# One fixed TensorE order in an attention stage: parts of one tile mode next to each other, zero-padded last rows, operations over two heads

## Chip, cores and metric

The program runs on one core of one Trainium2 chip. The metric is the device time of one execution in microseconds (us). Before the change it is 1012.68 us, the median of 3 runs (1012.34 to 1013.3).

## What is computed

Attention by feature maps, and behind it two feed-forward layers. The change lies in the attention alone; its shapes are 4 batches, 8 heads, 576 positions and a head size of 64, with 128 features.

```python
def phi(x):
    proj = np.einsum('bhsd,df->bhsf', x, w_phi)
    proj = proj - np.max(np.abs(proj), axis=-1, keepdims=True)
    return np.concatenate([np.exp(proj), np.exp(-proj)], axis=-1)
q_p, k_p = (phi(q), phi(k))
kv = np.einsum('bhsf,bhsd->bhfd', k_p, v)
z = np.sum(k_p, axis=2)
num = np.einsum('bhsf,bhfd->bhsd', q_p, kv)
den = np.einsum('bhsf,bhf->bhs', q_p, z)[..., None] + 1e-06
x = num / den            # then tokens x 512
x = relu(x @ w_in)**2 @ w_out
x = (sigmoid(x @ w_gate) * (x @ w_val)) @ w_out2
```

## The kernel before

The attention is a loop of 16 iterations, n = 0 to 15, one for each pair of heads (4 batches, NJ = 4 pairs each). An iteration touches three pairs at once, as a software pipeline: it transposes q and k of pair n+2 (`trans`, lines 298, 305 and 313), projects pair n+1 (`proj_k` line 347, `proj_q` line 326), forms the key sums of pair n (`kv`: line 373 for k_p times v, line 380 for the sums z by a column of ones) and transposes them (`kv_tr`, line 390), and forms denominators (line 403) and numerators (line 410) of pair n-1 (`num`). Of the 576 keys of a head, 512 are four chunks of 128 rows; the other 64 (the "last rows") of eight heads are packed two by two into the 128 partitions of `vr` and of the tile `phr`, and each pair of heads uses one half of these partitions.

The operands do not fill the TensorE array, so its instructions work on parts of it. The profile writes the part of an instruction as rows*columns: `128*64` means that two independent column halves exist, `128*32` four column quarters, `64*128` two row halves. Below this is called the tile mode. Each plain fp32 matmul of the program is two MATMUL instructions in the trace; an fp32r matmul and a transpose are one.

The other engines serve these matmuls. ScalarE (ACT) copies results out of PSUM (lines 289, 329, 382, 383, 392) and takes the exponentials (lines 338, 339 for q, 354, 355 for k). VectorE (DVE) subtracts the high part of a transposed tile (line 290), finds and subtracts maxima (lines 352, 353, and line 337 for q), transposes the denominators (line 414), inverts them (416, 417), spreads them (427) and multiplies (430). GpSimd (POOL) finds the maxima for q over partitions (line 331) and moves the inverted denominators (line 424). For q these operations act on half a head (288 columns), for k on one head (512 columns). In ten of the iterations (`CONVERTING`) DVE also runs one weight conversion of four operations of 512 columns (lines 111 to 116) for the feed-forward part; in four others it splits a part of the attention's result into high and low (`xsplit`, lines 95 and 96).

PSUM has eight one-bank tiles of 512 columns in this stage (`bank`). The order of instructions on each engine is set while the program is built, by a scheduler that follows the order of the code as far as data and buffers allow in its own model; at run time each engine takes its instructions strictly in that order. `tc.issue_after` puts an instruction behind another one of the same engine. Behind the loop the attention's PSUM tiles are given back and the feed-forward part begins at line 530.

Of the kernel before, what the change touches and what calls it, by code (L numbers as in the profile page):

```python
# [19 lines left out]
def attention_moe_moe2(ctx, tc, q, k, v, w_phi, w_in, w_out, w_gate, w_val, w_out2, out):  # L20
# [196 lines left out]
    with ExitStack() as actx:  # L217
# [25 lines left out]
        ones = cst.tile([P, 32], F32, name="ones")  # L243
        nc.vector.memset(ones, 1.0)
# [14 lines left out]

        nat = {}  # L260

        def load_rem(b):
# [3 lines left out]
            vr = lv.tile([P, 2, 2, D], F32, tag="vr", name="vr", bufs=2)  # L266
            for a in range(2):
                nc.sync.dma_start(out=vr[a * SR:(a + 1) * SR].rearrange("p g e d -> p (g e) d"),
                                  in_=v[b, 4 * a:4 * a + 4, SM:S, :].rearrange("h p d -> p h d"))
# [17 lines left out]
        def split_evac(pst, nm, key, bufs):  # L287
            t = tp.tile([P, 2, pst.shape[1]], F32R, tag=nm, name=nm, bufs=bufs)
# [4 lines left out]
        def trans_k(b, j):  # L293
            pt = bank(512)
            a = nat["k", b, j]
            for c in range(4):
                e, r = divmod(c, 2)
                nc.tensor.transpose(pt[:, c * P:(c + 1) * P], a[:, e, 2 * r:2 * r + 2, :], ident)  # L298
            split_evac(pt, "kT", ("k", b, j), 2)

        def trans_q(b, h):
            pt = bank(SH)
            a = nat["q", b, h // 2]
            for r in range(3):
                nc.tensor.transpose(pt[:, r * P96:(r + 1) * P96], a[:, h % 2, 2 * r:2 * r + 2, :], ident[:P96, :P96])  # L305
            split_evac(pt, "qT", ("q", b, h), 4)

        def trans_rem(b):
            a = nat["kr", b]
            pt = bank(NJ * SR)  # L310
            for j in range(NJ):
                o = (j % 2 * 2 + j // 2) * SR
                nc.tensor.transpose(pt[:, o:o + SR], a[:, 2 * j:2 * j + 2, :], ident[:SR, :SR])
# [4 lines left out]


        def proj_q(b, h):  # L320
            t = tT["q", b, h]
            pps = [bank(SH) for e in range(2)]
            for n, (x, y) in enumerate(passes):
                for e in range(2):
                    sl = slice(e * D, (e + 1) * D)
                    nc.tensor.matmul(pps[e], lhsT=wq[sl, x, :], rhs=t[sl, y, :], start=n == 0, stop=n == 2)  # L326
            for e in range(2):
# [4 lines left out]
                qx[b, h, e] = a  # L332
                mx[b, h, e] = m

        def q_exp(b, h, e):
            a = qx[b, h, e]
            nc.vector.tensor_tensor(a[:, 1, :], a[:, 1, :], mx[b, h, e], ALU.subtract)
# [5 lines left out]
        def proj_k(t, o, key, tag, bufs):  # L343
            pp = bank(512)
            for r in range(2):
                for n, (x, y) in enumerate(passes):
                    nc.tensor.matmul(pp[:, r * 256:(r + 1) * 256], lhsT=t[:, x, o + r * P:o + (r + 1) * P],  # L347
                                     rhs=wk[:, y].rearrange("p a f -> p (a f)"), start=n == 0, stop=n == 2)
            a = pp.rearrange("p (c f) -> p c f", c=4)
            t = php.tile([P, 4, 2, F], F32, tag=tag, name=tag, bufs=bufs)  # L350
# [503 lines left out]
```

## Time and profile before

| | us |
|---|---|
| median of 3 runs | 1012.68 |
| the profiled execution | 1013.1 |
| its span in the profile | 1011.3 |
| attention stage, up to the first matmul of line 530 | 198.4 |
| the rest | 812.9 |
| TensorE busy in the span | 991.6 (98%) |
| VectorE busy in the span | 747.3 (74%) |
| ScalarE busy in the span | 601.7 (59%) |

The profile shows one execution. A line of a timeline gives the start, the duration from the first start to the last end, the engine (PE is TensorE's matmuls, PEld its weight loads), the line of the kernel, the operation and its operands, and in brackets the idle time before it and what ended that. Instructions of one engine overlap a little at their ends, so the price of a group on a busy engine is the distance from its start to the start of the next. A line of the windows gives the window, its length, the busy time and, in brackets, the instructions of PE, PEld, DVE, ACT and POOL in this order, the granted TensorE clock (1.00 is 2.4 GHz, and the lower level, 1.2 GHz, is 0.50), the share of the DMA engines and GB/s.

### The profile page before, as it was taken

How to read it: one execution, taken by the hardware profiler on the slowest of the kernel's cores; microseconds unless marked ns; L12 is line 12 of the kernel's file. 1: busy time of each engine (PE TensorE's matmuls, PEld its weight loads, DVE VectorE, ACT ScalarE, POOL GpSimd, SP SyncE). 2: the span in 40 equal slices, each digit the busy share in tenths (PEclk: the TensorE clock that was granted, in tenths of full speed). 3: DMA queues.
4: the chain of work that ended last, by engine and by line, in shares of the span. 5: the costliest groups of instructions: out<-in, count | busy, mean ns of one | idle time of the engine just before them, and what ended most of it. 6: DMA issues, size and time to landing. Idle time of an engine off the chain costs nothing.

```text
span 1011.3 us, 17524 instructions
## 1 busy us (share of the span) xinstructions
PE 991.6 (98%) x6488; PEld 870.3 (86%) x6488; DVE 747.3 (74%) x1296; ACT 601.7 (59%) x1081; POOL 109.7 (11%) x196
## 2 busy tenths in 40 slices
PE   7999999999999999999999999999999999999996
PEld 6666666599999999889998899998899988999985
DVE  6799998869885987986969769856565656566532
ACT  6888878556555786446864466654465644555431
POOL 4556655400000000000000000000000000000000
PEclk9999999999999999999999999999999999999999
DMA  9444521349984576565775556632444422544302
GB/s 236 127 134 141 160 76 57 113 156 351 304 293 141 183 254 191 167 200 186 260 226 171 177 167 205 189 118 74 118 142 133 124 77 64 166 125 135 96 11 62
DMA packets 116406, 159.56 MB, mean 158 GB/s; under 512 B 12768, under 2 KB 74848, under 8 KB 116320
## 3 DMA queue, kind: packets, MB, share of 16 engines
q1 hardware_dynamic: 115680, 157.58, 49.8%
q8 instruction: 51, 0.84, 0.3%
q10 hardware_dynamic: 640, 0.85, 0.2%
q14 instruction: 35, 0.29, 0.1%
HBM read 125.37 MB, written 33.03 MB: 157 GB/s over the span
## 4 chain that ended last, share of the span: by engine, by line
PE 94%; DVE 3%; ACT 2%; POOL 0%; issue 0%; ACTq 0%
PE d L603 38%; PE d L551 20%; PE d L707 15%; PE d L530 7%; PE a L373 3%; PE a L410 3%; PE a L347 2%; PE a L380 2%; PE a L403 2%; PE a L326 1%; PE a L305 1%; PE a L390 1%; PE a L298 1%; ACT qe L329 0%; PE a L258 0%; ACT c L609 0%
## 5 line engine op out<-in xcount | busy, mean ns | idle before, releaser
L603 PE MATMUL d<-xs,hl 128*128 128x384 f32 x2184 | 385.4, 337 | 3.6 <-ACT c L609 3.6
L603 PEld LDWEIGHTS d<-xs,hl 128*128 128x128 f32 x2184 | 379.4, 188 | 6.6 <-ACT c L609 4.9
L138 DVE TENSOR_TENSOR hl<-wf,hl 128x512 fp32r<-128x512 f32 x282 | 192.4, 687 | 75.5 <-ACT hl L137 74.5
L137 ACT ACTIVATE hl<-wf 128x512 fp32r<-128x512 f32 x282 | 175.0, 626 | 88.5 <-PE d L603 48.3
L551 PE MATMUL d<-ghi,hl 128*128 128x256 f32 (+1 forms) x768 | 190.7, 338 | 0.0
L551 PEld LDWEIGHTS d<-ghi,hl 128*128 128x128 f32 x768 | 131.8, 188 | 16.3
L551 PE MATMUL d<-glo,hl 128*128 128x512 f32 (+1 forms) x384 | 128.5, 338 | 0.0
L707 PE MATMUL d<-hl,ghi 128*128 128x512 f32 x432 | 126.7, 395 | 0.0
L93 ACT ACTIVATE ghi<-G 128x768 fp32r<-128x768 f32 x48 | 40.7, 847 | 99.3 <-PE d L707 56.0
L707 PEld LDWEIGHTS d<-hl,ghi 128*128 128x128 f32 x432 | 80.9, 188 | 18.2
L96 DVE TENSOR_TENSOR glo<-G,ghi 128x768 fp32r<-128x768 f32 x48 | 46.0, 958 | 57.4 <-ACT ghi L93 56.9
L609 ACT ACTIVATE c<-d 128x768 f32<-128x768 f32 x78 | 61.3, 809 | 44.8 <-PE d L603 44.6
L331 POOL PARTITION_ALL_REDUCE m<-qe x64 | 83.5, 1375 | 35.5 <-ACT qe L329 33.3
L632 DVE TENSOR_TENSOR c<-c,d 128x768 f32<-128x768 f32 x54 | 51.2, 953 | 41.1 <-ACT c L609 26.8
L551 PEld LDWEIGHTS d<-glo,hl 128*128 128x128 f32 x384 | 72.3, 188 | 8.6
L707 PE MATMUL d<-hl,glo 128*128 128x512 f32 x216 | 76.3, 395 | 0.0
L530 PE MATMUL d<-xs,hl 128*128 128x384 f32 x384 | 69.1, 337 | 0.0
L530 PEld LDWEIGHTS d<-xs,hl 128*128 128x128 f32 x384 | 66.7, 188 | 1.1 <-issue 0.4
L115 ACT ACTIVATE st<-st 128x512 f32<-128x512 f32 x68 | 45.5, 678 | 32.4 <-DVE w L112 29.8
L707 PEld LDWEIGHTS d<-hl,glo 128*128 128x128 f32 x216 | 40.6, 188 | 9.8
L112 DVE SCALAR_TENSOR_TENSOR w<-st,w 128x512 uint32<-128x512 uint32 x68 | 46.6, 698 | 0.2
L113 DVE SCALAR_TENSOR_TENSOR w<-st,w 128x512 uint32<-128x512 uint32 x68 | 46.4, 693 | 0.5
(109 smaller groups left out, 1134.4 us busy)
## 6 DMA issues: line engine op xcount, KB each, us to landing
wf<-wd SPq DMA_DIRECT2D x84, 256.0 KB, 3.0
wf<-smd SPq DMA_DIRECT2D x72, 256.0 KB, 3.1
st<-in_moe_w_out_dram SPq DMA_DIRECT2D x28, 512.0 KB, 5.2
wf<-gvd SPq DMA_DIRECT2D x54, 256.0 KB, 3.2
wf<-wid SPq DMA_DIRECT2D x46, 256.0 KB, 4.3
st<-in_moe_w_in_dram SPq DMA_DIRECT2D x16, 512.0 KB, 5.9
wf<-ismd SPq DMA_DIRECT2D x32, 256.0 KB, 3.2
wd<-w SPq DMA_DIRECT2D x28, 256.0 KB, 3.4
```

Of the source, the lines that this page charges most:

```text
L96: last_g[0] = nc.vector.tensor_tensor(lo, src, f(hi), ALU.subtract)
L112: nc.vector.scalar_tensor_tensor(b, hi, 0xC0000000, b, ALU.bitwise_and, ALU.bitwise_or)
L113: nc.vector.scalar_tensor_tensor(b, lo, 29, b, ALU.logical_shift_right, ALU.bitwise_or)
L137: nc.scalar.activation(d[:, 0], a, AF.Copy)
L138: nc.vector.tensor_tensor(d[:, 1], a, f(d[:, 0]), ALU.subtract)
L331: nc.gpsimd.partition_all_reduce(m, a[:, 1, :], channels=P, reduce_op=bass_isa.ReduceOp.absmax)
L530: nc.tensor.matmul(pp[:, i, :n], lhsT=w[:, x, j, :], rhs=xs[j][:, y, o:o + n], start=k == 0, stop=k == 3 * NJ - 1)
L551: nc.tensor.matmul(acc[j][i], lhsT=w[:, x, j, :], rhs=a[y][:, o:o + n], start=c == 0 and k == 0 and (i == 0 or j % 2 == 0), stop=c == C1 - ...
L603: nc.tensor.matmul(acc[k, q][:, m], lhsT=w[:, i, 2 * m + kt, :], rhs=v[:, j, kt, :], start=start and n == 0, stop=n == 5, skip_group_check ...
L609: nc.scalar.activation(side[name, q], acc["X", q], AF.Copy)
L632: nc.vector.tensor_tensor(a, a, acc[k, q], ALU.add)
L707: nc.tensor.matmul(acc[u], lhsT=g[x][:, u * P:(u + 1) * P], rhs=w[:, y].rearrange("p j f -> p (j f)"), start=c == 0 and n == 0, stop=c == ...
```

## The change

The code of an iteration is put in another order, the TensorE instructions of the attention are kept in the order of the code (`pin`), `kv` is divided into `zsum` and `kv`, and `num` into `den` and `num`. The last rows use all 128 partitions, with zeros in the half of `vr` (or of the column of ones) that belongs to other heads. Operations on q act on a whole head or on two, on k on two heads; the results of q's transposes and projections and of `num` lie in tiles of two PSUM banks. `xsplit` takes its high part on ScalarE. In the new loop the transposes stand first.

```diff
-    ps = pctx.enter_context(tc.tile_pool(name="ps", bufs=8, space=PSUM))
+    ps = pctx.enter_context(tc.tile_pool(name="ps", bufs=4, space=PSUM))
+    def two():
+        return ps.tile([P, 2, 512], F32, tag="b", name="b", bufs=2)
...
-        for o, n in HALVES:
-            split(a[:, 0, o:o + n], a[:, 1, o:o + n], xy_tile(0, j)[:, o:o + n])
+        split(a[:, 0], a[:, 1], xy_tile(0, j), nc.scalar)
...
+        pin = tc.keep_in_program_order
...
-            vr = lv.tile([P, 2, 2, D], F32, tag="vr", name="vr", bufs=2)
+            vr = lv.tile([P, 2, 4, D], F32, tag="vr", name="vr", bufs=2)
             for a in range(2):
+                nc.gpsimd.memset(vr[(1 - a) * SR:(2 - a) * SR, a], 0.0)
...
-            for e in range(2):
-                a = qpp.tile([P, 2, SH], F32, tag="qe", name="qe", bufs=12)
-                nc.scalar.activation(a[:, 1, :], pps[e], AF.Copy)
-                m = qpp.tile([P, SH], F32, tag="m", name="m", bufs=4)
-                nc.gpsimd.partition_all_reduce(m, a[:, 1, :], channels=P, reduce_op=bass_isa.ReduceOp.absmax)
+            a = qpp.tile([P, 2, 2 * SH], F32, tag="qe", name="qe", bufs=6)
+            nc.scalar.activation(a[:, 1].rearrange("p (i n) -> p i n", i=2), pps, AF.Copy)
+            m = qpp.tile([P, 2 * SH], F32, tag="m", name="m", bufs=2)
+            nc.gpsimd.partition_all_reduce(m, a[:, 1], channels=P, reduce_op=bass_isa.ReduceOp.absmax)
...
+        def zsum(b, j):
+            kz = bank(3 * F)
+            for r, e, a, t in phis(b, j):
+                for u in range(2):
+                    o = 32 * (2 * e + u)
+                    pin(nc.tensor.matmul(kz[o:o + 32, 2 * F:], lhsT=ones[:, 0 if r < 4 else 1 + a], rhs=t[:, u],
+                                     start=r == 0, stop=r == 4))
...
         def kv(b, j):
+            for r, e, a, t in phis(b, j):
+                l = vx[:, e, r, :] if r < 4 else vr[:, a, 2 * (j % 2) + e, :]
+                pin(nc.tensor.matmul(kz[e * D:(e + 1) * D, :2 * F], lhsT=l, rhs=t.rearrange("p u f -> p (u f)"),
+                                 start=False, stop=r == 4, skip_group_check=True))
             kt = sm.tile([P, 3, F], F32, tag="kvt", name="kvt", bufs=2)
-            nc.scalar.activation(kt[:, 0:2].rearrange("p u f -> p (u f)"), pk, AF.Copy)
-            nc.scalar.activation(kt[:, 2], pz, AF.Copy)
+            nc.scalar.activation(kt.rearrange("p u f -> p (u f)"), kz, AF.Copy)
...
             for h in (2 * j, 2 * j + 1):
-                for i in range(2):
-                    q_exp(b, h, i)
+                q_exp(b, h)
+            before = divmod(n - 1, NJ)
+            if n + 2 < B * NJ:
+                trans_q(*divmod(n + 2, NJ))
+            if n + 2 < B * NJ:
+                trans_ks(n + 2)
+            if n:
+                kv_tr(*before)
             if n + 1 < B * NJ:
                 proj_ks(n + 1)
                 proj_qs(n + 1)
-            if n + 2 < B * NJ:
-                trans(n + 2)
+            if n:
+                den(*before)
+            zsum(b, j)
+            if n:
+                num(*before)
             kv(b, j)
-            if n:
-                num(*divmod(n - 1, NJ))
-            kv_tr(b, j)
             if n + 1 == B * NJ:
+                kv_tr(b, j)
+                den(b, j)
                 num(b, j)
```

How the orders move. First TensorE in one iteration in the middle, before (lines of the kernel before; 373 and 380 are `kv`, 403 and 410 `num`, 390 `kv_tr`, 347 and 326 the projections, 305 and 298 the transposes; here a row of line 373, 380, 403 or 410 counts matmuls of the program):

```order
L373 MATMUL a<-ph,vx 64x256 x8
L373 MATMUL a<-phr,vr 64x256 x2
L380 MATMUL a<-ph,ones 32x128 x16
L380 MATMUL a<-phr,ones 32x128 x4
L403 MATMUL a<-qe,kvs 32x288 x8
L410 MATMUL a<-qe,kvs 64x288 x8
L390 MATMUL a<-ident,kvt 128x128 x3
L347 MATMUL a<-wk,kT 128x256 x12
L326 MATMUL a<-qT,wq 128x288 x12
L305 MATMUL a<-ident,q 128x96 x6
L298 MATMUL a<-ident,k 128x128 x4
```

and the same now (lines of the changed kernel; 314 and 306 are the transposes, 403 `kv_tr`, 357 and 334 the projections, 418 `den`, 383 `zsum`, 444 `num`, 393 `kv`):

```order
L314 MATMUL b<-ident,q 128x96 x6
L306 MATMUL a<-ident,k 128x128 x4
L403 MATMUL a<-ident,kvt 128x128 x3
L357 MATMUL a<-wk,kT 128x256 x12
L334 MATMUL b<-qT,wq 128x288 x12
L418 MATMUL a<-qe,kvs 32x288 x8
L383 MATMUL a<-ph,ones 32x128 x16
L383 MATMUL a<-phr,ones 32x128 x4
L444 MATMUL b<-qe,kvs 64x288 x8
L393 MATMUL a<-ph,vx 64x256 x8
L393 MATMUL a<-phr,vr 64x256 x2
```

The work is the same; the two kinds with 32 output rows now stand together, and so do the two with 64. `kv_tr` used to have the eight matmuls of `num` and the denominators between itself and its `kv`; now only the transposes stand there.

Second ScalarE, which feeds `kv_tr`, over one iteration of the changed kernel (396 copies the result of `kv` for `kv_tr`, 345 and 346 are the exponentials for q, 297 the copies of the transposes, 405 the copy behind `kv_tr`, 336 the copies of q's projection, 364 and 365 the exponentials for k, 117 a weight conversion):

```order
L396 ACTIVATE kvt<-a 128x384
L297 ACTIVATE qT<-b 128x576
L297 ACTIVATE kT<-a 128x512
L405 ACTIVATE kvs<-a 128x384
L345 ACTIVATE qe<-qe 128x576
L346 ACTIVATE qe<-qe 128x576
L336 ACTIVATE qe<-b 128x576 x2
L364 ACTIVATE ph<-ph 128x8x128
L117 ACTIVATE st<-st 128x512
L365 ACTIVATE ph<-ph 128x8x128
L345 ACTIVATE qe<-qe 128x576
L346 ACTIVATE qe<-qe 128x576
```

The copy of line 396 comes next after the last of these rows: it stands right behind two exponentials for q, which need DVE's subtraction (line 344). Third VectorE, over the same stretch of the changed kernel (361 and 362 are maxima and subtraction for k, 450 the final product, 113 to 118 the weight conversion, 422 the transposed denominators, 424 and 425 their inverse, 344 the subtraction for q, 298 the low parts of the transposes, 434 the spread denominators):

```order
L361 TENSOR_REDUCE km<-a 128x4 x2
L450 TENSOR_TENSOR u<-b,rr 128x576
L113 TENSOR_SCALAR w<-st 128x512
L362 TENSOR_TENSOR ph<-a,km 128x4x128 x2
L114 SCALAR_TENSOR_TENSOR w<-st,w 128x512
L422 STREAM_TRANSPOSE den<-a 128x288
L115 SCALAR_TENSOR_TENSOR w<-st,w 128x512
L424 TENSOR_SCALAR rd<-den 128x9
L344 TENSOR_TENSOR qe<-qe,m 128x576
L118 SCALAR_TENSOR_TENSOR w<-st,w 128x512
L425 RECIPROCAL rd<-rd 128x9
L344 TENSOR_TENSOR qe<-qe,m 128x576
```

Before, four operations of 288 columns stood for the two of line 344, and the conversion's operations stood between them in the same way. At the end of the loop TensorE has, in the changed kernel, for the last pair:

```order
L393 MATMUL a<-phr,vr 64x256 x2
L403 MATMUL a<-ident,kvt 128x128 x3
L418 MATMUL a<-qe,kvs 32x288 x8
L444 MATMUL b<-qe,kvs 64x288 x8
L563 MATMUL d<-xs,hl 128x384 x72
```

Here each of the first three rows needs a copy by ScalarE of what the row above it made; before, the denominators and numerators of pair 14 stood between `kv` and `kv_tr` of pair 15.

## Rows read from the trace of the kernel before

**Rows 1.** Windows: the attention, the rest, and stretches at its start and end

```profile
0.00:198.50 198.50, 190.63 (x2121) 126.34 (x2121) 170.53 (x387) 156.05 (x383) 109.02 (x193) 0.99 0.48 133
198.50:1011.30 812.80, 800.95 (x4370) 743.95 (x4368) 576.78 (x909) 445.66 (x698) 0.70 (x4) 1.00 0.51 164
...
24.05:28.70 4.65, 4.65 (x27) 3.82 (x27) 3.31 (x6) 4.33 (x12) 0.46 (x1) 0.63 0.88 195
...
175.82:198.44 22.62, 21.94 (x251) 12.28 (x250) 18.04 (x41) 15.10 (x35) 11.69 (x32) 1.00 0.42 140
190.00:198.44 8.44, 7.86 (x99) 3.78 (x92) 5.07 (x14) 3.25 (x7) 2.83 (x16) 1.00 0.01 2
8.00:22.60 14.60, 13.53 (x145) 10.40 (x143) 12.95 (x26) 12.79 (x33) 10.03 (x8) 1.00 1.14 264
```

**Rows 2.** Timeline of TensorE's matmuls over one iteration (n = 8)

```profile
111.05 1.95 PE L373 MATMUL a<-ph,vx 128*64 128x256 f32 x16
112.93 0.65 PE L373 MATMUL a<-phr,vr 64*64 64x256 f32 x4
113.51 1.08 PE L380 MATMUL a<-ph,ones 128*32 128x128 f32 x32
114.52 0.42 PE L380 MATMUL a<-phr,ones 64*32 64x128 f32 x8
114.87 1.18 PE L403 MATMUL a<-qe,kvs 128*32 128x288 f32 x16
115.98 2.16 PE L410 MATMUL a<-qe,kvs 128*64 128x288 f32 x16
118.07 0.55 PE L390 MATMUL a<-ident,kvt 128*128 128x128 f32 x3
...
119.95 1.07 PE L326 MATMUL a<-qT,wq 64*128 64x288 f32 x12
121.12 0.77 PE L305 MATMUL a<-ident,q 96*128 96x96 f32 x6
...
122.31 1.95 PE L373 MATMUL a<-ph,vx 128*64 128x256 f32 x16
```

**Rows 3.** Timeline: an early line 326 and what follows it; weight load behind 119.95

```profile
38.73 1.07 PE L326 MATMUL a<-qT,wq 64*128 64x288 f32 x12
39.73 0.71 PE L305 MATMUL a<-ident,q 96*128 96x96 f32 x6
...
121.12 0.58 PEld L305 LDWEIGHTS a<-ident,q 96*128 96x128 f32 x6 [0.33 <-ACT qe L329]
```

**Rows 4.** Windows: the iteration that follows, with a weight conversion

```profile
111.12:122.38 11.26, 11.16 (x131) 7.27 (x133) 10.46 (x25) 9.42 (x25) 6.85 (x14) 1.00 0.50 144
```

**Rows 5.** Timeline of VectorE in that iteration

```profile
112.71 0.81 DVE L290 TENSOR_TENSOR qT<-a,qT 128x288 fp32r<-128x288 f32 x2
113.44 0.69 DVE L112 SCALAR_TENSOR_TENSOR w<-st,w 128x512 uint32<-128x512 uint32 x1
114.04 0.99 DVE L337 TENSOR_TENSOR qe<-qe,m 128x288 f32<-128x288 f32 x1
...
119.36 0.69 DVE L352 TENSOR_REDUCE km<-a 128x4 f32<-128x512 f32 x1 [0.76 <-PE a L347]
```

**Rows 6.** Timeline of ScalarE in that iteration

```profile
118.46 0.44 ACT L339 ACTIVATE qe<-qe 128x288 f32<-128x288 f32 x1
118.81 0.47 ACT L392 ACTIVATE kvs<-a 128x384 f32<-128x384 f32 x1
```

**Rows 7.** Timeline of TensorE: three waits for ScalarE, two early, one late

```profile
14.69 0.73 PE L347 MATMUL a<-wk,kT 128*128 128x256 f32 x4 [1.07 <-ACT kT L289]
...
24.05 0.44 PE L390 MATMUL a<-ident,kvt 128*128 128x128 f32 x2 [1.40 <-ACT kvt L382]
...
195.24 1.18 PE L403 MATMUL a<-qe,kvs 128*32 128x288 f32 x16 [0.58 <-ACT kvs L392]
```

**Rows 8.** Timeline of GpSimd: the maxima of one iteration

```profile
109.96 5.27 POOL L331 PARTITION_ALL_REDUCE m<-qe  x4 [0.89 <-ACT qe L329]
```

More of the change, by code (lines that the diff above doesn't have):

```diff
@@ L242, in attention_moe_moe2 @@
         split(wq[:, 0], wq[:, 1], wst)
-        ones = cst.tile([P, 32], F32, name="ones")
-        nc.vector.memset(ones, 1.0)
+        ones = cst.tile([P, 3, 32], F32, name="ones")
+        nc.vector.memset(ones, 0.0)
+        nc.vector.memset(ones[:, 0], 1.0)
+        for a in range(2):
+            nc.vector.memset(ones[a * SR:(a + 1) * SR, 1 + a], 1.0)
         zr = cst.tile([P, F], F32, name="zr")
@@ L297, in trans_k, with trans_q @@
                 e, r = divmod(c, 2)
-                nc.tensor.transpose(pt[:, c * P:(c + 1) * P], a[:, e, 2 * r:2 * r + 2, :], ident)
+                pin(nc.tensor.transpose(pt[:, c * P:(c + 1) * P], a[:, e, 2 * r:2 * r + 2, :], ident))
             split_evac(pt, "kT", ("k", b, j), 2)
[L301 to L306, printed above, removed]
+        def trans_q(b, j):
+            pt = two()[:, :, :SH]
+            a = nat["q", b, j]
+            for e in range(2):
+                for r in range(3):
+                    pin(nc.tensor.transpose(pt[:, e, r * P96:(r + 1) * P96], a[:, e, 2 * r:2 * r + 2, :], ident[:P96, :P96]))
+            split_evac(pt, "qT", ("q", b, j), 2)
         def trans_rem(b):
@@ L354, in proj_k, with phis @@
             nc.scalar.activation(t[:, :, 0, :], t[:, :, 1, :], AF.Exp)
             nc.scalar.activation(t[:, :, 1, :], t[:, :, 1, :], AF.Exp, scale=-1.0)
-            ph[key] = t
+            return [t[:, 4 * e:4 * e + 4] for e in range(ne)]
         kvs = {}
         kts = {}
+        def phis(b, j):
+            a, g = divmod(j, 2)
+            for r in range(5):
+                for e in range(2):
+                    yield r, e, a, ph[b, 2 * j + e][:, r] if r < 4 else ph["r", b][:, 2 * g + e]
@@ L367, in kv @@
[L367 to L380 removed]
+            kz = kts[b, j]
@@ L393, in kv_tr, with den @@
             kvs[b, j] = ks
-        def num(b, j):
+        rds = {}
+        def den(b, j):
             ks = kvs[b, j]
@@ L424, in num, with trans_ks @@
                         nc.gpsimd.tensor_copy(r[o:o + 32, i], rd[q:q + 32])
-            for i in range(2):
-                rr = sm.tile([P, nb, 32], F32, tag="rr", name="rr", bufs=2)
-                nc.vector.transpose(rr, r[:, i, :].unsqueeze(2).to_broadcast([P, nb, 32]))
-                rr = rr.rearrange("p a b -> p (a b)")
+            rr = sm.tile([P, 2 * nb, 32], F32, tag="rr", name="rr", bufs=2)
+            nc.vector.transpose(rr, r.rearrange("p i n -> p (i n)").unsqueeze(2).to_broadcast([P, 2 * nb, 32]))
+            rds[b, j] = rr.rearrange("p (i a) b -> p i (a b)", i=2)
+        def num(b, j):
+            ks = kvs[b, j]
+            pn = two()[:, :, :SH]
+            for i in range(2):
+                for u in range(2):
+                    for e in range(2):
+                        o = u * P + e * D
+                        pin(nc.tensor.matmul(pn[e * D:(e + 1) * D, i], lhsT=ks[:, o:o + D],
+                                         rhs=qx[b, 2 * j + e][:, u, i * SH:(i + 1) * SH], start=u == 0, stop=u == 1))
+            rr = rds.pop((b, j))
+            whole = list(cols(b * S, S))
+            if len(whole) == 1:
+                po, m, t, o = whole[0]
+                last[0] = nc.vector.tensor_tensor(xy_tile(t, j)[:, o:o + S].rearrange("p (i n) -> p i n", i=2), pn, rr, ALU.mult)
+                return
+            for i in range(2):
                 for po, m, t, o in cols(b * S + i * SH, SH):
-                    last[0] = nc.vector.tensor_tensor(xy_tile(t, j)[:, o:o + m], pn[i][:, po:po + m],
-                                                      rr[:, po:po + m], ALU.mult)
+                    last[0] = nc.vector.tensor_tensor(xy_tile(t, j)[:, o:o + m], pn[:, i, po:po + m],
+                                                      rr[:, i, po:po + m], ALU.mult)
         def trans(n):
+            trans_q(*divmod(n, NJ))
+            trans_ks(n)
+        def trans_ks(n):
             b, j = divmod(n, NJ)
-            for e in range(2):
-                trans_q(b, 2 * j + e)
             trans_k(b, j)
```

88 lines of the change are left out of this document (34 added, 54 removed).

## Prediction

> **What bounds the kernel now.** I read the windows first [rows 1]. In the attention (0 to 198.5 us) TensorE is busy for 190.63 us, 96%, but VectorE stands close behind it with 170.53 us (86%) and ScalarE with 156.05 (79%). Behind it TensorE is busy for 800.95 of 812.80 us, and the change touches no instruction there; what the attention ends earlier, the program ends earlier, and I cost the rest at nothing. Then the timeline of one iteration [rows 2]: kv of n = 8 starts at 111.05, that of n = 9 at 122.31, so an iteration takes 11.26 us, and TensorE goes from group to group without a wait. The time to win is inside the groups and at their borders. The window of the next iteration [rows 4] is the one to keep in mind: VectorE is busy 10.46 of 11.26 us in an iteration with a weight conversion, and what it has left is one wait of 0.76 us for TensorE [rows 5].
>
> **What a border costs.** In [rows 2] the same instruction stands in two groups of different length. Line 373: 16 instructions take 1.88 us (111.05 to 112.93), 4 take 0.58. The difference, 12 in 1.30 us, is 0.108 us each; the rest, 1.88 - 16 x 0.108 = 0.15 us, is a fixed price per group. Line 380: 32 in 1.01, 8 in 0.35, so 0.0275 each and 0.13 fixed. At each of these starts the tile mode is another one. I take 0.14 us per change of mode.
>
> **TensorE in the loop.** Before, an iteration has nine changes of mode: `128*64`, `64*64`, `128*32`, `64*32`, `128*32`, `128*64`, `128*128`, `64*128`, and back to the full columns for the transposes. Now it has four: transposes, kv_tr and k's projection in one mode, q's projection, den and zsum, num and kv. Five fewer are 5 x 0.14 = 0.70 us. The zero rows cost nothing on TensorE: the last rows are still 4 and 8 instructions with the same number of columns. A second piece: line 326 to line 305 takes 1.17 us (119.95 to 121.12), in an early iteration 1.00 (38.73 to 39.73); the weight load there has idle time that ends with ScalarE's copy of line 329, which frees the PSUM tile of the transpose [rows 2, 3]. The transposes no longer follow that projection: 0.17 us. Together 0.87 us per iteration, so 10.39 in place of 11.26. Iterations 2 to 13 are complete ones: 12 x 0.87 = **-10.4 us**.
>
> **The loop through VectorE and ScalarE.** The merged operations save these two only what an instruction costs beside its columns. On VectorE two of 288 columns take 0.73 us (112.71 to 113.44), one of 512 takes 0.60 (113.44 to 114.04) [rows 5]; per column (0.60 - 0.365)/224 = 1.05 ns, so one of 576 takes 0.67, and a merge saves 0.06. Five merges per iteration (qT, two of line 337, rr, the product; in batches 1 and 2 the product stays in pieces) are 0.3 us: 10.46 becomes 10.2 against 10.39 of TensorE. VectorE has no time left for waits, and the new order has them. kv_tr comes 1.2 us behind its kv (the transposes, 121.12 to 122.31, stand between [rows 2]); before, denominators and numerators did, over 3 us. kv_tr needs the copy kvt on ScalarE, which stands behind two exponentials for q, which need VectorE's subtraction of the first head. Around that loop, an operation of 512 columns at 0.60: two maxima 1.2, product 0.67, conversion 0.6, two subtractions for k 1.2, conversion 0.6, den 0.4, conversion 0.6, rd 0.2, subtraction for q 0.67, makes 6.1; with the one operation that is stretched while POOL searches maxima (0.91 from 114.04 in place of 0.37 [rows 5, 8]) 6.6. Then ScalarE: 0.1 to start and two exponentials at 0.57 (0.35 for 288 columns, 118.46 to 118.81 [rows 6], and the same slope as above), 1.25; kvt 0.4; the copy of the transposed q with its way 0.8; back on VectorE qT, kT and rr, 0.67 + 0.6 + 0.7. That is 11.0 us, 0.6 more than TensorE needs. It binds where VectorE has its conversion, in nine of the twelve iterations; the iterations n = 3 and 7 have another 1.2 us of VectorE for the last rows against some 0.7 of TensorE. In full this is 9 x 0.6 + 2 x 0.5 = 6.4 us; nothing, if lag is carried into the three iterations without a conversion. In part of the iterations the order has rr ahead of qT, and the loop is shorter; the first ones are absorbed by up to 1 us of lag. I take **+2.3**, with 0 and 6.4 as ends. The Trainium skill (TensorEngine Tiling (Array Packing), PSUM Bottleneck) says that tiling speeds up TensorE but not the emptying of PSUM, which may then bound; by that rule alone the full 6.4 would be paid. The windows, with 9.42 us of ScalarE and 10.46 of VectorE in 11.26 [rows 4], put it near that limit and not beyond.
>
> **Start.** TensorE waits 1.07 us at 14.69 and 1.40 at 24.05, and behind the second the granted clock is 0.63 over 4.65 us, which costs 4.65 x 0.37 = 1.7 us [rows 1, 7]. The transposes of pairs 2 and 3 now stand ahead of these places and fill them, but the copies waited for stand behind exponentials of 1024 columns. Iterations 0 and 1 save some 1.4 in borders. If both holes close and the clock stays up: -5.6. If a hole of the same size comes on top, +2. I take **-1.0**, nearer to the borders alone.
>
> **End.** From 175.82 the last two iterations take 22.62 us [rows 1]. The wait at 195.24 is the bare price of one copy out of PSUM with ScalarE free: 0.58 [rows 7]. With no transposes left, kv_tr waits bare in n = 14, twice in n = 15 and den twice: five in place of one, +2.3; eight borders fewer, -1.1; a lower clock in between perhaps, 0.3 on average. **+1.5**, between -1.1 (the copies hide) and +4.6 (1.7 lost twice beside 1.2).
>
> **What costs nothing.** POOL's maxima go from 4 x 1.32 us [rows 8] to two of 576 columns, together between 2.6 and 5.3 if the price lies between fixed and per column; more is not excluded, but POOL is busy for 6.85 of 11.26 us [rows 4] and has about 4 in hand. Its eight memsets of zeros, at most a maximum each (1.3 us), lie in the same gap, twice in four iterations. xsplit's high part moves to ScalarE, four times 768 columns, 0.35 + 480 x 0.00105 = 0.85 us each by the price of 288 [rows 6] and the slope above, in the 1.8 us that ScalarE has free per iteration, and VectorE wins it in iterations without a conversion. SP issues the same loads.
>
> **Sum.** -10.4 - 1.0 + 1.5 + 2.3 = -7.6 us. Against the profiled execution, 1013.1, that is 1005.5; it stood 0.4 above the median, so against the median **1005.1**. A measurement of this kernel can tell 0.2%, 2 us, from no change.
>
> **Rivals.**
> *No new wait*: lag is carried, the early holes close. -10.4 - 2.5 + 0.3 = -12.6: 1000.1. For it: waits of TensorE are rare before, and lag had 0.76 us per iteration. Chance 0.20.
> *The loop binds throughout*: -10.4 - 1.0 + 1.5 + 6.4 = -3.5: 1009.2. For it: 10.2 against 10.39 with waits on top. Against it: the schedule alternates. Chance 0.18.
> *The fixed price belongs to every new group of instructions, not to a change of mode*. Then only the two last-row groups go, since they follow their like: 2 x 0.14 + 0.17 = 0.45 per iteration, -5.4, with -0.6, +1.7 and, since TensorE is slower, only +0.8 of the loop: -3.5, 1009.2. Against it: two kinds of group show the same 0.14. Chance 0.08.
> *Waits drop the clock: slower*. The place is kv_tr in the iterations with a conversion. A stall of 0.87 us eats what an iteration wins; over nine of them 1.1 us each makes the whole change a loss. If each stall reaches 1.40, as at 24.05, the clock falls as it did there: 1.4 + 1.7 = 3.1 each, 9 x 3.1 - 10.4 - 1.0 + 1.5 = +18: 1030.7. Against it: the loop is 0.6 too long, not 1.4, and waits of 0.58 and 1.07 [rows 7] were not followed by such a fall: the windows around them show 1.00 [rows 1]. Chance 0.12. The Trainium skill (TensorE: Matmul & The Clock Gate, A second HAM failure mode) reports a kernel in which short idle times between groups, while PSUM buffers are cycled, made the clock go up and down; the change has two big buffers where eight small ones were. By that rule shorter waits than 1.4 us would do, and the time would be near 1031.
>
> **How the numbers follow.** The forecast has 0.42. Faster by over 2 us are the forecast, the first rival, and most of the second and third: 0.42 + 0.20 + 0.18 = 0.80. The other 0.08 of these two lie within 2 us; slower is the last, 0.12. The range runs from below the first rival, since the start may give more, to beyond the second: 998.5 to 1012.5, leaving out the slower rival and a little below.
>
> **What would show it.** Right: four fixed prices per iteration in TensorE's timeline, no gap between den and zsum or num and kv, iterations near 10.4 us without a conversion and 10.4 to 11 with one, and kv_tr waiting for kvt in some of these. Four waits of about 0.6 in the last iteration. Wrong: a gap of 0.14 between den and zsum (third rival), no wait at kv_tr (first), a granted clock below 1.00 in the loop (last), or waits of TensorE for a load of q or k at the start.

## The result, and the profile after

The change makes the kernel slower: 1022.55 us (median of 4 runs, 1021.93 to 1023.76) against 1012.81 for the kernel before (4 runs), ratio 1.0098 with a 95% interval of 1.008 to 1.0115. The span grows from 1011.3 to 1020.7 us, by 9.4. The windows of the changed kernel (columns as in [rows 1]): the attention, the rest, an iteration without a wait, one with waits, the end from its last kv but two onward, and a stretch in it.

```profile
0.00:206.67 206.67, 182.07 (x2120) 130.73 (x2121) 163.11 (x311) 143.43 (x227) 105.63 (x168) 0.99 0.46 128
206.67:1020.70 814.03, 801.60 (x4370) 744.18 (x4368) 575.92 (x904) 446.15 (x698) 0.76 (x4) 1.00 0.51 164
57.83:68.09 10.26, 10.26 (x131) 7.57 (x129) 8.48 (x15) 7.09 (x13) 6.17 (x12) 1.00 0.59 172
92.12:105.46 13.34, 11.48 (x138) 8.31 (x136) 11.09 (x24) 10.09 (x16) 6.76 (x10) 1.00 0.42 122
178.59:206.67 28.08, 22.19 (x251) 13.89 (x250) 16.57 (x29) 14.49 (x25) 11.56 (x30) 0.94 0.36 114
193.50:198.00 4.50, 4.39 (x62) 3.02 (x64) 1.89 (x6) 0.63 (x2) 1.49 (x8) 0.62 0.00 0
```

TensorE's busy time in the attention falls from 190.63 [rows 1] to 182.07 us, and still the attention ends 8.2 us later: TensorE was idle for 7.9 us of it before and is idle for 24.6 us now. All three engines have time left in the slow iteration too (13.34 us, VectorE busy for 11.09, ScalarE for 10.09); none of them is the bound, the way between them is. TensorE's timeline of an iteration (n = 6 to 7; columns as in [rows 2]) shows both halves of the story:

```profile
92.12 1.90 PE L393 MATMUL a<-ph,vx 128*64 128x256 f32 x16
93.85 0.60 PE L393 MATMUL a<-phr,vr 128*64 128x256 f32 x4
94.38 0.71 PE L314 MATMUL b<-ident,q 96*128 96x96 f32 x6
94.93 0.60 PE L306 MATMUL a<-ident,k 128*128 128x128 f32 x4
96.65 0.55 PE L403 MATMUL a<-ident,kvt 128*128 128x128 f32 x3 [1.12 <-ACT kvt L396]
...
99.27 0.67 PE L334 MATMUL b<-qT,wq 64*128 64x288 f32 x6
100.67 0.66 PE L334 MATMUL b<-qT,wq 64*128 64x288 f32 x6 [0.74 <-ACT qe L336]
101.27 1.18 PE L418 MATMUL a<-qe,kvs 128*32 128x288 f32 x16
102.26 1.06 PE L383 MATMUL a<-ph,ones 128*32 128x128 f32 x32
103.14 0.40 PE L383 MATMUL a<-phr,ones 128*32 128x128 f32 x8
103.47 2.16 PE L444 MATMUL b<-qe,kvs 128*64 128x288 f32 x16
```

kv's first 16 instructions take 1.73 us to the next start (1.88 in [rows 2]), and the 32 of the sums 0.88 (1.01): no border lies there any more. But kv_tr waits 1.12 us for the copy of its tile, and the second head of q's projection waits 0.74 for ScalarE's copy of q's projection, which has to free one of the two big PSUM tiles. The other one does not help here. VectorE multiplies the numerators of the pair before, and so empties their tile, only from 101.51 on, after the second head has begun at 100.67:

```profile
101.51 0.87 DVE L454 TENSOR_TENSOR u<-b,rr 128x192 f32<-128x192 f32 x3
```

In all six iterations of the loop with this wait the product starts between 0.02 us ahead of the second head and 0.95 us behind it; in the other six it starts ahead of the first head. The trace does not tell the two big tiles apart; that the late product holds the other one is read from this. ScalarE over the first of these waits, that of kv_tr:

```profile
92.78 1.06 ACT L364 ACTIVATE ph<-ph 128x1024 f32<-128x1024 f32 x1 [2.39 <-DVE ph L362]
93.87 1.06 ACT L365 ACTIVATE ph<-ph 128x1024 f32<-128x1024 f32 x1
94.84 0.67 ACT L345 ACTIVATE qe<-qe 128x576 f32<-128x576 f32 x1
95.53 0.68 ACT L346 ACTIVATE qe<-qe 128x576 f32<-128x576 f32 x1
96.12 0.47 ACT L396 ACTIVATE kvt<-a 128x384 f32<-128x384 f32 x1
```

kv is done at 94.4, but its copy starts at 96.12, behind three exponentials (0.67 and 0.68 us for a head of q; half a head took 0.44 in [rows 6]). These exponentials began late themselves: ScalarE was idle for 2.39 us ahead of line 364, for VectorE's subtraction for k (line 362). Between 36 and 176 us it is so 12 times, 16.0 us in all. So VectorE has a part in the way that makes the copy late. TensorE's waits between 34.55 and 178.59, twelve iterations (us in total, times, longest):

```profile
PE b L334 <- ACT qe L336: 4.5, 6, 0.7
PE a L403 <- ACT kvt L396: 2.3, 4, 1.1
PE a L418 <- DVE kT L298: 1.9, 3, 0.7
PE a L383 <- DVE ph L362: 1.9, 2, 1.3
PE a L357 <- ACT kvs L405: 0.9, 2, 0.4
PE b L334 <- DVE qT L298: 0.9, 1, 0.9
```

And the end, with the kind of wait that [rows 7] has once, at 195.24:

```profile
192.02 0.55 PE L403 MATMUL a<-ident,kvt 128*128 128x128 f32 x3 [2.22 <-ACT kvt L396]
193.61 1.52 PE L418 MATMUL a<-qe,kvs 128*32 128x288 f32 x16 [1.04 <-ACT kvs L405]
...
202.35 0.55 PE L403 MATMUL a<-ident,kvt 128*128 128x128 f32 x3 [0.59 <-ACT kvt L396]
203.47 1.18 PE L418 MATMUL a<-qe,kvs 128*32 128x288 f32 x16 [0.58 <-ACT kvs L405]
```

Ahead of the longest of them, 2.22 us, ScalarE does this:

```profile
188.83 1.13 ACT L139 ACTIVATE hl<-wf 128x512 fp32r<-128x512 f32 x2
189.87 0.67 ACT L346 ACTIVATE qe<-qe 128x576 f32<-128x576 f32 x1
190.44 1.15 ACT L139 ACTIVATE hl<-wf 128x512 fp32r<-128x512 f32 x2
191.49 0.47 ACT L396 ACTIVATE kvt<-a 128x384 f32<-128x384 f32 x1
```

kv is done at 189.8. Ahead of its copy stand not only exponentials but also the copies of line 139, which split the first weights of the feed-forward part into high and low.

To sum up by place, I cut both traces where the same work is done (kv, den and num of an iteration ended, the next kv_tr not begun), at n = 1 and n = 13. Kernels of the experiments follow in the same table; "loop" is twelve iterations. The four parts are of the profiled execution, the median is of all runs; the profiled execution of x11 lies 0.8 us below its median, that of x15 1.9.

| kernel | start | loop | end | rest of the span | median, us |
|---|---|---|---|---|---|
| before | 36.84 | 138.98 | 22.62 | 812.9 | 1012.81 |
| changed | 34.55 | 144.04 | 28.08 | 814.0 | 1022.55 |
| x14_end_only | 34.54 | 144.01 | 27.81 | 814.2 | 1022.54 |
| x12_kv_then_num | 34.57 | 142.74 | 23.56 | 813.1 | 1016.40 |
| x15_one_bank_end | 34.39 | 140.35 | 28.17 | 813.2 | 1020.13 |
| x11_kv_then_num_one_bank | 33.10 | 134.77 | 22.06 | 813.2 | 1006.09 |

Of the 9.4 us, -2.3 are the start, +5.1 the loop, +5.5 the end, +1.2 the rest (0.59 of it a wait of the first feed-forward matmul for the last product). Twelve iterations at 10.26 us would be 123.1, and with the 3.9 that the loop before has beyond 12 x 11.26 (the last rows, above all) 127.0. So some 17 us of waits fill the loop; the profile names 12.4 of them. By this estimate the others lie inside groups that it counts as busy, as in line 334 at 111.07, which takes 1.42 us in place of 1.06.

### The profile page after: what moved, and what is told of

Same layout as the page of the kernel before. It is cut to its first block, busy times and chain, and to the rows that moved or that the text cites. A ratio compares the mean times of both kernels' runs of the same rounds, so it can differ in the third digit from the quotient of the medians.

```text
span 1020.7 us, 17232 instructions
## 1 busy us (share of the span) xinstructions
PE 983.7 (96%) x6488; PEld 874.9 (86%) x6488; DVE 739.0 (72%) x1215; ACT 589.6 (58%) x925; POOL 106.4 (10%) x172
## 4 chain that ended last, share of the span: by engine, by line
PE 83%; DVE 10%; ACT 4%; POOL 1%; issue 1%; ACTq 0%; POOLq 0%; DVEq 0%
PE d L636 37%; PE d L584 20%; PE d L740 15%; PE d L563 6%; DVE km L361 1%; POOL rc L432 1%; DVE ph L362 1%; PE a L393 1%; DVE w L114 1%; PE b L444 1%; DVE rr L434 1%; DVE qT L298 1%; PE a L383 1%; DVE u L454 1%; DVE kT L298 1%
## 5 line engine op out<-in xcount | busy, mean ns | idle before, releaser
L338 POOL PARTITION_ALL_REDUCE m<-qe x32 | 70.2, 2241 | 66.0 <-ACT qe L336 32.8
L114 DVE SCALAR_TENSOR_TENSOR w<-st,w 128x512 uint32<-128x512 uint32 x68 | 50.4, 753 | 0.2
L118 DVE SCALAR_TENSOR_TENSOR w<-st,w 128x512 f32<-128x512 f32 x68 | 46.1, 684 | 1.1 <-ACT st L117 0.2
```

The source lines that it names most:

```text
L114: nc.vector.scalar_tensor_tensor(b, hi, 0xC0000000, b, ALU.bitwise_and, ALU.bitwise_or)
L118: nc.vector.scalar_tensor_tensor(a, h, TINY, a, ALU.is_ge, ALU.mult)
L338: nc.gpsimd.partition_all_reduce(m, a[:, 1], channels=P, reduce_op=bass_isa.ReduceOp.absmax)
```

## The experiments

The kernel before stood at 1012.7 to 1012.95 us each time that it was measured beside them. For kernels outside the table above the loop is given from kv of n = 1 to kv of n = 13, the same twelve iterations: 138.99 before, 144.04 after.

**One cure at a time.** Three theories: the two-bank tiles make the waits (A), or kv_tr's place 1.2 us behind kv does (B), or the fixed order itself is the price (C). For A, every PSUM tile is one bank again, out of one ring of eight. What was read out of a big tile in one operation (transposed q, projected q, the numerators) is then read half by half, so this edit changes the tiles and the length of these reads together:

```diff
-    ps = pctx.enter_context(tc.tile_pool(name="ps", bufs=4, space=PSUM))
+    ps = pctx.enter_context(tc.tile_pool(name="ps", bufs=8, space=PSUM))
...
-        return ps.tile([P, 2, 512], F32, tag="b", name="b", bufs=2)
+        return [bank(SH) for i in range(2)]
...
-            nc.scalar.activation(a[:, 1].rearrange("p (i n) -> p i n", i=2), pps, AF.Copy)
+            for i in range(2):
+                nc.scalar.activation(a[:, 1, i * SH:(i + 1) * SH], pps[i], AF.Copy)
...
```

> The changed kernel with its order, pins, zero rows and whole-head operations on SBUF kept, but the two-bank PSUM tiles replaced by pairs of one-bank tiles out of eight (transposed q, projected q and the numerators are then copied out, or multiplied, half by half). Theory A, PSUM tiles: TensorE waits in the loop since too few and too big PSUM tiles are handed on (the second head of q's projection waits 0.74 us for the copy of the first in six iterations, den, zsum and k's projection wait for subtractions and copies in seven more places); then nearly all waits but those at kv_tr go, and the time falls by 7 to 11 us, to 1012 to 1016. Theory B, the short way from kv to kv_tr through ScalarE's queue: the waits stay or move to kv_tr, 1018 to 1023. Theory C, the strict order itself: no difference, 1020 to 1024.

1021.48 us, loop 141.87: in the ranges of B and C. The wait for q's copy falls from 4.5 to 1.1 us, that of kv_tr grows from 6.6 to 10.1 over the whole attention:

```profile
PE a L408 <- ACT kvt L401: 10.1, 11, 1.8
...
PE a L338 <- ACT qe L341: 1.1, 3, 0.4
```

For B, kv_tr behind proj_ks:

```diff
-            if n:
-                kv_tr(*before)
             if n + 1 < B * NJ:
                 proj_ks(n + 1)
+            if n:
+                kv_tr(*before)
+            if n + 1 < B * NJ:
                 proj_qs(n + 1)
```

> The changed kernel with one move: kv_tr stands behind k's projection in place of ahead of it, 1.6 us later, so that the copy it needs has more time. Theory A: only the waits at kv_tr go (2.3 us in iterations 1 to 13, and some of the end), the waits for PSUM tiles stay: 1018 to 1021. Theory B: the loop through ScalarE was what held TensorE, the other waits are its echo: 1008 to 1014. Theory C: no difference, 1020 to 1024.

1025.09, loop 150.81: above all three ranges. The wait for kvt goes from the loop (3.1 us in two places at the end stay), and kv_tr now waits for its PSUM bank, which k's transposes hold until VectorE has read them: 11.4 us in four waits.

```profile
104.22 0.83 PE L403 MATMUL a<-ident,kvt 128*128 128x128 f32 x3 [4.37 <-DVE kT L298]
```

Neither A nor B holds by itself. For C, without the fixed order (pin returns its argument) the scheduler moves groups apart again:

> The changed kernel without the pins: the scheduler may move matmuls again, all else as changed. It then puts other groups between the two heads of q's projection and so changes the tile mode more often (8 to 11 times per iteration in the order I see, in place of 4). Theory C: the fixed order is the price, TensorE's waits go and the time is 1008 to 1014. Theories A and B: waits for PSUM tiles or for kv_tr get shorter by what is put in between, but each border costs 0.14 us, so little is won: 1016 to 1024.

1017.92, loop 138.35: in the range of A and B, above that of C. 4.6 us are won back, and kv_tr's wait stands at 9.1 us.

**The gain by itself.** The kernel before with the zero-padded rows, den beside zsum and kv beside num, and nothing else (half-head operations, eight one-bank tiles, transposes behind the projections, no pins). The order, without the zero padding:

```diff
-            kv(b, j)
+            if n:
+                den(*divmod(n - 1, NJ))
+            zsum(b, j)
+            kv(b, j)
             if n:
                 num(*divmod(n - 1, NJ))
```

> The kernel before with the tile-mode part of the change alone: last rows zero-padded, denominators and key sums next to each other, kv and numerators next to each other (kv ahead, so that numerators still stand between kv and kv_tr); no pins, eight one-bank tiles, operations of half a head, transposes where they were. By the price of a border, 0.14 us, four changes of mode fewer per iteration in fifteen iterations give -8 us: 1003 to 1006, if the waits of the changed kernel come from its PSUM tiles (A) or from the transposes standing first (B). If a border does not cost that, or if VectorE becomes the bound as soon as TensorE is faster, 1009 to 1013.

1012.75 (ratio 0.9997, 0.9987 to 1.0006): in the range that I had given for a border that costs nothing or for VectorE as the bound. But the loop is 134.12 us, 4.9 shorter (four borders of 0.14 in twelve iterations would be 6.7), and everything is lost at the end, where den of pair 14 now stands bare behind its own kv_tr:

```profile
182.06 0.55 PE L397 MATMUL a<-ident,kvt 128*128 128x128 f32 x3 [1.49 <-DVE hl L138]
185.32 2.15 PE L412 MATMUL a<-qe,kvs 128*32 128x288 f32 x16 [2.72 <-ACT kvs L399]
```

The same with the last iteration put in another order (zsum and kv of pair 15 ahead of den of pair 14):

> x4_modes_only with one move: in the last iteration den and num of the pair before stand behind zsum and kv, so that the copy of kvs has work of TensorE beside it. The loop is the same (10.7 us an iteration). If the end alone gave back what the loop had won: from the last kv but one to the first feed-forward matmul 19.5 to 20.5 us (22.63 in x4_modes_only, 19.56 in the kernel before), and the kernel takes 1009 to 1011 us, faster than both. If the end is set by VectorE and ScalarE, whatever the order: 1012 to 1013.

1009.33 (0.9967, 0.9954 to 0.998): faster than before, and the first feed-forward matmul starts at 195.22 in place of 198.88, behind a wait of 1.75 for the last product. From the last kv but one it is 19.17 us, just under the 19.5 to 20.5 expected. The theory of the end held.

**Order or operations?** The changed kernel's operations and tiles in the order of before, then the old operations and tiles in the new order:

> The changed kernel's operations and tiles (whole heads, two-bank tiles, zero-padded rows, pinned), in the order of the kernel before: proj_ks, proj_qs, trans, den, zsum, kv, num, kv_tr. If the new order alone makes the cycle: the loop's period falls to some 10.7 us as in x4_modes_only, and the time to 1011 to 1015 us, the waits at the end as in x4_modes_only. If the operations over two heads or the two-bank tiles alone make it: the period stays near 11.8 and the time at 1019 to 1024. If it takes both: 1011 to 1015 here and in x8_new_order_old_ops.

> x4_modes_only (half-head operations, eight one-bank tiles, zero-padded rows, mode groups side by side) with the changed kernel's order: trans, kv_tr, proj_ks, proj_qs, den, zsum, num, kv, pinned. If the new order alone makes the cycle: period near 11.8 us and 1018 to 1024 us, waits at kv_tr and kT. If the larger operations or tiles alone make it: period 10.3 to 10.8, no more than 3 us of waits at kv_tr in the loop, and 1008 to 1014 us.

1023.59 (loop 143.85) and 1021.07 (loop 140.50): neither is cured, so none of the three cases that I had written down came out; each half is slow, and each with other waits. In x8 nearly all waits of the loop are kv_tr's, 6.9 of 8.0 us (14.4 in 15 places over the whole attention). In x7 most are those of the big tiles, 7.3 of 11.9 us in the loop, which ScalarE's copies and VectorE's product have to free; over the whole attention:

```profile
PE b L334 <- DVE u L454: 3.0, 4, 1.1
PE b L334 <- DVE u L450: 2.5, 3, 1.1
PE b L314 <- ACT qe L336: 2.3, 6, 0.6
```

To tell tiles from operations there, x7 with one-bank tiles (and the last iteration of x5):

> x7_old_order with one-bank tiles (operations over whole heads otherwise kept) and the last iteration as in x5_modes_end. If the two-bank tiles made x7_old_order slow: the loop runs at 10.7 to 11.0 us an iteration as in x5_modes_end and the kernel takes 1005 to 1010 us. If the operations over whole heads made it: 1014 to 1021.

The loop falls to 135.28 us, 8.6 shorter and near the 134.07 of x5, which was the sign that I had given for the tiles. The time, 1013.81 (1012.08 to 1015.94), misses the forecast for either case: the first feed-forward matmul starts at 196.78, after a wait of 2.7 us for the last product, and the runs scatter. By the loop it is the tiles, with the shorter reads that come with them.

**VectorE's load.** The ten weight conversions in iterations 1 to 3 and 8 to 14:

> The changed kernel with the ten weight conversions in iterations 1 to 3 and 8 to 14 in place of 1 to 8, 10 and 12, so that iterations 4 to 7 have none. A conversion puts four operations (about 3 us) on VectorE and one on ScalarE. If that load is what makes the cycle too long: iterations 4 to 7 run at 10.3 to 10.7 us each, with no wait of TensorE over 0.3 us, and those with a conversion stay at 11.3 to 13. If the order of the kernel's own operations makes it: iterations 4 to 7 stay at 11.3 or more. The total is no test here: 1018 to 1028 by either.

1021.11. Without a conversion the four iterations take 11.85, 11.53, 11.97 and 10.26 us; with it they took 11.86, 12.17, 13.34 and 11.15. So 2.9 us of the 7.5 above four times 10.26 hang on the conversion, and an iteration with VectorE busy for 8.38 of 11.53 us is still late. The load makes the waits longer; it does not explain the rest.

**Both cures.** One-bank tiles, and kv_tr behind proj_ks:

> The changed kernel with both earlier cures at once: every PSUM tile one bank (eight of them) and kv_tr behind proj_ks, 2.5 us later than in the change. Theory of two separate waits (the two-bank PSUM tiles, about 5.5 us, and kv_tr behind the copy of its tile, about 6.6 us, each only let the other grow when it was cured alone): with both gone the loop runs at TensorE's own 10.3 to 10.7 us an iteration and the kernel takes 1010 to 1014 us. Theory of the cycle (the order of the work makes a round trip through VectorE, ScalarE and back longer than TensorE's own work, and the wait shows at whichever instruction comes first): the waits appear at a third place (kT, ph or the PSUM tile of kv_tr) and the time stays at 1019 to 1025 us.

1015.69, loop 136.32: between the two expectations, 1.7 above the range of two separate waits and 3.3 below that of the cycle. What made the time worse when done alone (x2: +2.5 us) makes it 5.8 better beside one-bank tiles. That pointed to a better way to give kvt time, with no group between other groups: num behind kv in place of ahead of it. Both have the same tile mode, so no border is added, and 2.0 us more of TensorE's work stand between kv and kv_tr. The last iteration as in x5.

```diff
-            if n:
-                num(*before)
             kv(b, j)
+            if n:
+                num(*before)
```

> x8_new_order_old_ops with num moved behind kv (den, zsum, kv, num, trans, kv_tr, proj_ks, proj_qs: no mode border more), so that 3.5 us of TensorE's work and no longer 1.3 stand between kv and the kv_tr that needs the copy of its tile; the last iteration as in x5_modes_end. Theory of the cover (in the change's order the copy of kvt, queued behind exponentials on ScalarE, has too little beside it): the waits of kv_tr fall from 14.4 us to under 3, the period to 10.3 to 10.8 us, the kernel takes 1003 to 1008 us. Theory of the cycle (any wait that is taken away comes up elsewhere): period 11 or more, 1012 to 1020.

> x1_one_bank (the change's whole-head operations, one-bank tiles) with the same two moves. Theory of the cover: 1004 to 1009 us, within 2 us of x10_kv_then_num_half; if the whole-head operations cost something of their own: 3 us or more above x10. Theory of the cycle: 1014 to 1021.

> The changed kernel with the same two moves and nothing else: two-bank tiles stay. Theory of the cover with the two-bank wait beside it: the waits at kv_tr go, those at the two-bank tiles of proj_q and trans_q (some 5 us) stay: 1009 to 1014 us. Theory of the cycle: 1017 to 1023. If the two-bank tiles cost nothing once the order is mended: within 2 us of x11_kv_then_num_one_bank.

With half-head operations 1011.90, with whole-head operations and one-bank tiles **1006.09** (0.9933, 0.9916 to 0.9949), with two-bank tiles 1016.40. The second is faster than both kernels, by 6.9 and 16.5 us, and the only one where the theory of the cover had it, though 5.8 below the first and not within 2. The first misses: kv_tr's waits fall from 14.4 to 3.7 us (under 3 was expected), but the time lies 3.9 above the range and the loop of 139.02, 11.6 an iteration, is what the theory of the cycle had named. The third lies between its two ranges. The waits of the second over the same twelve iterations, and its windows over this stretch and from there to the first feed-forward matmul:

```profile
PE a L423 <- ACT qe L341: 2.4, 7, 0.5
PE a L338 <- ACT qe L341: 1.1, 3, 0.4
PE a L408 <- ACT kvt L401: 0.2, 1, 0.2
```

```profile
28.85:163.62 134.77, 130.89 (x1583) 95.24 (x1579) 120.26 (x236) 104.33 (x204) 82.29 (x125) 1.00 0.43 120
163.62:189.93 26.31, 24.75 (x289) 15.07 (x285) 21.45 (x41) 18.11 (x31) 14.82 (x32) 1.00 0.37 122
```

VectorE is busy for 120.26 of 134.77 us in this loop, 89%, ScalarE for 77%, and TensorE goes on beside them. But its loop is only 4.2 us shorter than that of the kernel before, about half of what I had forecast for the loop (10.4 less 2.3). It lies 7.8 above the 127.0 us of a loop without waits, and the profile names 3.7 of these. The start gives another 3.7 us, the end 0.6. In x12 the wait for kvt has gone too (0.4 us in the loop), and those of the big tile remain: 4.8 us for q's copy, up to 0.9 each, and 3.2 for ph. The half-head operations (x10 against x11, loop 139.02 against 134.77) cost 4.3 us of loop; which of them was not tried.

The last two corners separate the last iteration from num's place:

> The changed kernel with the last iteration alone in the order of x12_kv_then_num (num stays ahead of kv in the loop, two-bank tiles stay). By the traces of the change and of x12 the end is worth 2.5 us (30.34 against 27.81 us from the last kv but two to the first feed-forward matmul): 1019 to 1021 us. What is left to x12's 1016.40 is then what num behind kv gives beside two-bank tiles.

> x1_one_bank with that last iteration alone: 32.84 us from the last kv but two to the feed-forward become some 27, so 1015 to 1018 us. What is left to x11's 1006.09 is what num behind kv gives beside one-bank tiles. Theory of two waits that cover each other: that is 8 us or more, against 4 or less beside two-bank tiles (x14_end_only against x12_kv_then_num). Theory of two costs that simply add: the two differences agree within 2 us.

1022.54 and 1020.13, both above their ranges: the last iteration alone is worth nothing beside two-bank tiles and at most 1.4 us beside one-bank tiles, where the runs scatter by more. Num behind kv is worth 6.1 us beside two-bank tiles (1022.54 to 1016.40) and 14.0 beside one-bank tiles (1020.13 to 1006.09); the tiles are worth 2.4 ahead and 10.3 behind. I had written 8 or more against 4 or less: the second bound is missed, the difference of 7.9 is not. Not all of this difference belongs to the two waits. By the spans of the profiled executions it is 6.4, and in x15 the first feed-forward matmul waits 2.70 us for the last product, which it does not do in x11. The loop is the cleaner test: there the one cure gives 1.3, the other 3.7, both 9.2. x1 and x15 have the same loop and took 141.87 and 140.35 us for it (in x1 the granted clock fell once), so some 1.5 us of such a difference can be scatter; the 4.3 by which both exceed the sum of the two is beyond that. In the end num's place counts most, 4.3 to 6.1 us (with the 2.70 in the second), because in n = 14 no transposes are left between kv and kv_tr, while ScalarE's queue holds the weight copies of line 139. In x14 one of these waited for the DMA of its weights, and the copy of kvt behind it with it (the first two lines here; the third is x15's first feed-forward matmul):

```profile
191.75 1.15 ACT L139 ACTIVATE hl<-wf 128x512 fp32r<-128x512 f32 x2 [1.26 <-DMA wf<-wid]
193.33 0.90 PE L403 MATMUL a<-ident,kvt 128*128 128x128 f32 x3 [3.58 <-ACT kvt L396]
...
202.91 12.75 PE L566 MATMUL d<-xs,hl 128*128 128x384 f32 x72 [2.70 <-DVE u L454]
```

The reading that fits all of these: an iteration contains two round trips from TensorE over ScalarE and back, kv's copy for kv_tr and the copy that frees a big tile for the second head while VectorE's product still holds the other. ScalarE takes its queue in order, as the lines above show. If one of the two no longer holds TensorE, TensorE comes earlier to the other, finds ScalarE as far as before, and waits there for most of what was won. That both edits are needed is shown; this reason for it is argued. No run moved the copy of kvt ahead of the exponentials in ScalarE's queue, or VectorE's product by itself, and the time that x10 lost inside its groups is not explained. A theory of a cycle that no cure shortens is out, since x11's loop is 9.3 us shorter than the change's, with 3.7 us of named waits in place of 12.4.

## Why the prediction was wrong, point by point

- **The border** was right. The one iteration of the change's loop without waits takes 10.26 us (11.26 before, 10.39 forecast), den and zsum follow each other without a gap, and the third rival is out.
- **The start** gave -2.3 where I took -1.0, inside its ends.
- **The step that failed is "I take +2.3, with 0 and 6.4 as ends".** The wait that I had in mind is there at just that size: kv_tr for kvt, 2.3 us in four places of the loop. That this size agrees is luck: with one-bank tiles (x15) the same wait in the same twelve iterations is 7.2 us. And the whole wait of the change's loop is some 17 us. I followed one loop, and never asked of the new PSUM tiles who frees them: four uses per iteration (q's transposes, two heads of the projection, num), two tiles, a copy of 0.65 us between the first and the second head, and in half of the iterations a product that comes too late to free the other tile. A wait of this kind stood in [rows 3], 0.33 us of a transpose for q's copy; I counted it only as something to win. x15 and x12 against x11 price the two in the presence of each other, 5.6 us of loop for num's place and 8.0 for the tiles (with the longer reads out of them). The sum of the loop that I did follow has a slip as well: by its own slope an exponential of 576 columns takes 0.65 us, not 0.57, and the trace has 0.67 and 0.68.
- The Trainium skill (TensorEngine Tiling (Array Packing), PSUM Bottleneck), by which TensorE gains and the emptying of PSUM stays, was weighed at 6.4 us. The traces agree with it in kind, and the bound was too small: x11, which empties the same data, is 9.3 us shorter in the loop, so what counts is TensorE's work ahead of the copy's result and the tiles with the way that they are read, not the emptying as such.
- **The end**: forecast +1.5, at most +4.6, measured +5.5. The five waits stand where I said (0.72 at 179.37, 2.22, 1.04, 0.59 and 0.58), but I priced each as a bare copy of 0.58 us. The copy of the second stood behind exponentials and weight copies (line 139), that of the third behind an exponential which ScalarE began 0.53 us late, for VectorE. Behind these two the granted clock was 0.62 for 4.5 us, which is some 1.7 us by 4.5 x 0.38.
- **The rest**, costed at nothing, grew by 1.2 us. Half of it is the wait for the last product (0.59); the other half is open.
- **What costs nothing**: the maxima of POOL are two of 2.24 us, inside their range; the profile names the split on ScalarE in no wait of TensorE's matmuls.

```profile
L338 POOL PARTITION_ALL_REDUCE m<-qe x32 | 70.2, 2241 | 66.0 <-ACT qe L336 32.8 <-DVE km L361 21.7 <-DVE kT L298 4.9
```

- **The rivals.** The sign was that of the slower one, its mechanism only in part: waits of kv_tr, but in the loop the clock stayed at 1.00 behind waits of up to 1.3 us. The Trainium skill's warning (TensorE: Matmul & The Clock Gate, A second HAM failure mode) of a clock that goes up and down while PSUM buffers are cycled does not show in the loop of the change. The one fall there, at the end, follows a wait of 2.22 us. The change does not have two big tiles in place of eight, either: four one-bank tiles stand beside them.

## What to carry to other kernels

Before TensorE is made faster in an iteration, list every place where it needs another engine's copy inside that iteration, for data and for the release of a PSUM tile alike, and compare the work of TensorE that lies between with the queue ahead of that copy, not with the copy alone. A queue ahead can hold work of another part of the program, and wait for another engine or a DMA itself. With several such places, curing one may show little (here 1.3 and 3.7 us of loop, 9.2 together): cure them together as well before calling one harmless. Longer operations and larger tiles are two edits: here the longer operations won 4.3 us of loop, and the larger tiles with the longer reads out of them cost 8.0.

## What was not expected of the hardware

The granted clock can fall behind single waits in the middle of a busy loop as well: to 0.57 between 119 and 123 us in x1 (behind 1.83 us) and to 0.66 between 104 and 109 in x2 (behind 4.37). But the length of the wait alone does not tell when. In x1 a wait of the same 1.83 us at 72.03 was followed by the full clock, in x2 waits of 2.42, 2.64 and 1.99, in x15 one of 2.82. x1 behind its two waits of 1.83 us:

```profile
72.03:76.03 4.00, 3.89 (x43) 3.13 (x47) 3.72 (x7) 3.87 (x10) 0.90 (x3) 1.00 0.98 290
119.36:123.36 4.00, 4.00 (x23) 3.78 (x25) 3.26 (x6) 2.69 (x6) 0.39 (x2) 0.58 1.04 305
```

In x4 it was 0.57 from 186 to 192 us, where TensorE counts as busy throughout, behind waits of 1.49 and 2.72:

```profile
186.00:192.00 6.00, 6.00 (x72) 3.67 (x62) 2.69 (x8) 0.69 (x2) 1.49 (x8) 0.57 0.00 0
```

So a busy share near 100% in a window does not say that the clock is up, and a wait's price can lie in the work behind it. A search for maxima over 576 columns took 2241 ns on POOL against 1375 for 288: 1.63 times as long for twice the columns.
